# The first transform step as two 64-column matmuls with signed tables, and weight stores issued from ScalarE's queue

## The chip, the cores and the metric

The kernel runs on one core of a Trainium2 chip. The metric is the device time of one execution in microseconds (us), from the first to the last instruction with what lies around them. The engines are TensorE (PE; its weight loads are shown as PEld), VectorE (DVE), ScalarE (ACT), GpSimd (POOL) and SyncE (SP), which here only issues DMAs.

## The reference

A long convolution, and two feed-forward layers on its result, for S = 12480 tokens of width D = 128:

```python
h_filt = (np.maximum(pos_emb @ w1, 0) @ w2) * np.exp(-0.01 * pos)[:, None]
u = x * v
y = irfft(rfft(u, n=2*S) * rfft(h_filt, n=2*S))[:S]       # per channel
a = x * y
h = a @ w_in;  a = (h * clip(h + 3, 0, 6) / 6) @ w_out    # d_ff = 2048
h = a @ w_in2; out = where(h > 0, h, exp(min(h, 0)) - 1) @ w_out2
```

All arrays are float32 on the host.

## The kernel before

The convolution is done with matmuls, as a Fourier transform of length 196 x 128 in two steps. The input is folded beforehand: position i and its mirror image lie side by side, so that the transform works on the sums (f = 0) and the differences (f = 1) of such pairs, 64 of each.

**Opening.** `filter_hidden` (L262) makes the hidden values of the filter: matmuls on TensorE, one VectorE instruction that applies relu and window (L269), and the sums and differences (L274, on VectorE or GpSimd). It writes them to `Rf`.

**First steps of the transform.** `first` (L293) transforms four channels at a time: four fp32 matmuls (L296), each with 98 x 128 stationary values (64 sums and 64 differences of one channel) and a 98 x 198 table `t1` as the moving operand. The result `pa` (PSUM; the pool `ps` has four buffers) has the sums in partitions 0 to 63 and the differences in 64 to 127. Both went through the same table, and the differences need its columns with real and imaginary part exchanged and one sign changed. So the result is written to SBUF by three instructions: L300 copies the upper half (ScalarE, 792 elements), L301 copies one part of the lower half (ScalarE, 396), L302 multiplies the other by -1 (VectorE, 396). `first` runs 32 times in what is called stage 1 here (16 times for the signal into `Au`, `au` in the profile, and 16 for the filter into `Ar`, part of `qb`), and 16 times more in stage 3.

The signal's input comes from `signal` (L252): three GpSimd instructions (L255 multiplies x and v, L257 and L258 make sums and differences) into one of three buffers. Its loads are issued by SP: `ld` from `in_xc` (L215) and `qb` from `in_vc` (L206).

**The stages.** Stage 1 is the list `steps` (L407). Stage 2, `second_all(0)`, runs over groups of four frequencies, two groups at a time: `second_r` (L324; ScalarE copies its result, L327), `second_u` (L316), `second_h` (L331); then per group ScalarE copies half of the result `z` (L336, `ta`), VectorE makes two products (L338, `tb` and `tc`), and GpSimd their sums (L344). Stage 3 (L420) runs `third` for the first half of the channels (PE L353, a ScalarE copy L357, two VectorE instructions L359) in turn with `first` and `signal` for the second half. Stage 4 is `second_all(1)`. Then come `third` for the second half, `fourth` (L452) and the feed-forward layers (from L514 on; matmuls L575 and L619), which take most of the time.

`fourth` has matmuls with 64 stationary columns (99 x 64) that write to partitions 0 to 63 or 64 to 127 of `y`; the two halves are issued in turn by its inner loop.

**The weights.** The feed-forward weights arrive as 64-bit floats, and VectorE makes 32-bit floats of them in 32 jobs: `weight_steps` (L147) is a generator with three steps a job (L172 to L174; L176 and L177; L181 and L182), of integer and float instructions on 256 columns. After the second step of job k it issues the store of job k-1 to DRAM (L162, from `rs`, three buffers) and the load of job k+2 (L157), both on SP's queue. `convert(n)` (L191) takes n steps on average, and is called after each `first` in stage 1 (1.1 steps), after each group of stage 2 (1.5), each round of stage 3 (1.5) and each group of stage 4 (0.6). Every engine and queue works through its instructions in the order in which this program issues them; there is no other scheduler.

The lines that the change touches:

Of the kernel before, what the change touches and what calls it, by code (L numbers as in the profile page):

```python
# [9 lines left out]
F32 = mybir.dt.float32  # L10
# [5 lines left out]
ALU = mybir.AluOpType  # L16
# [5 lines left out]
H1 = N1 // 2  # L22
NK = H1 + 1
HN = N2 // 2
# [24 lines left out]
def tables():  # L49
    n1, k1, k2 = np.arange(H1), np.arange(NK), np.arange(N2)  # L50
    i, m, a = np.arange(HN), np.arange(NM), np.arange(H1) - 2 * SHIFT - 1
    w = 2 * np.pi * (np.outer(n1 - SHIFT, k1) % N1) / N1
    t1 = np.stack([np.cos(w), -np.sin(w)], axis=2)
    k = k1[:, None] + N1 * k2
    w = np.pi * (((2 * i + 1)[:, None, None] * k) % (2 * L)) / L
    gm = np.concatenate([np.cos(w), np.sin(w)], axis=0)

    w = 2 * np.pi * (np.outer(k2, m) % N2) / N2
    c, s = np.cos(w), np.sin(w)
    cs = np.stack([  # L60
        np.concatenate([c[:, :HN], s[:, 1:HN], c[:, HN:]], axis=1),
        np.concatenate([c[:, :1], s[:, 1:HN], c[:, 1:]], axis=1),
    ], axis=1)
    w = 2 * np.pi * (np.outer(k1, a) % N1) / N1
    pa = np.stack([np.cos(w), -np.sin(w), np.sin(w), np.cos(w)], axis=1)
    ends = (m == 0) | (m == HN)
    w = 2 * np.pi * np.outer(k1, m) / L - np.where(ends, np.pi / 4, 0.0)
    c = np.outer(np.where((k1 == 0) | (k1 == H1), 1.0, 2.0) / L, np.where(ends, np.sqrt(0.5), 1.0))
    pm = np.stack([np.cos(w), np.sin(w)], axis=2) * c[:, :, None]
    win = folded(np.exp(-0.01 * np.arange(S, dtype=np.float32))[:, None])[:, 0].transpose(0, 2, 1)  # L70
    return [np.ascontiguousarray(z, dtype=np.float32) for z in (t1, gm, cs, pa, pm, win)]


def folded(z):

    z = np.pad(z, ((0, SP - S), (0, 0))).reshape(H1, N2, -1)
    return np.stack([z[:, HN:], z[:, HN - 1::-1]], axis=1).transpose(0, 3, 1, 2)
# [3 lines left out]
def tile_kernel(ctx, tc, xc, vc, xT, posT, w1_d, w2_d, moe_w, t1_d, gm_d, cs_d, pa_d, pm_d, win_d, outT):  # L81
    nc = tc.nc
    w_dram = [nc.dram_tensor(f"w_scratch{i}", (128, FF), F32, kind="Internal").ap() for i in range(4)]
# [15 lines left out]
    const = sctx.enter_context(tc.tile_pool(name="const", bufs=1, side="right"))  # L99
# [4 lines left out]
    WC = 256  # L104
# [30 lines left out]
    def load_pos(n):  # L135
        for c in (slice(a * H1, b * H1) for a, b in list(zip(edges, edges[1:]))[n]):
            nc.sync.dma_start(pos_t[:, c], posT[:, c])

    load_pos(slice(0, 3))
    t1 = const.tile([H1, 2 * NK], F32, name="t1")  # L140
    nc.scalar.dma_start(t1, t1_d)
    cs = const.tile([128, 2 * N2], F32, name="cs")
    nc.scalar.dma_start(cs, cs_d)
    nc.scalar.dma_start(w2s.rearrange("p h x -> p (h x)"), w2_d)
# [2 lines left out]
    def weight_steps():  # L147
        v = nc.vector
        jobs = [(i, c) for i in range(4) for c in range(0, FF, WC)]
        raws = [spare[:, :2 * WC], spare[:, 2 * WC:4 * WC], late[:, 3 * VT:]]  # L150
        e, rs = spare[:, 4 * WC:5 * WC], [spare[:, (5 + i) * WC:(6 + i) * WC] for i in range(3)]
        ei = e.bitcast(I32)

        def load(k):
            if k < len(jobs):
                i, c = jobs[k]
                nc.sync.dma_start(raws[k % 3].bitcast(I64), moe_w[i][:, c:c + WC])  # L157

        def store(k):
            if k >= 0:  # L160
                i, c = jobs[k]
                nc.sync.dma_start(w_dram[i][:, c:c + WC], rs[k % 3])  # L162

        load(0)
        load(1)
        yield
        for k in range(len(jobs)):
            r32 = raws[k % 3].rearrange("p (n t) -> p n t", t=2)
            lo_w, hi_w = r32[:, :, 0].bitcast(U32), r32[:, :, 1].bitcast(I32)
            r = rs[k % 3]  # L170
            ri = r.bitcast(I32)
            v.tensor_scalar(ei, hi_w, 20, 0x7FF, op0=ALU.logical_shift_right, op1=ALU.bitwise_and)  # L172
            v.tensor_scalar(ri, hi_w, 0xFFFFF, 0x100000, op0=ALU.bitwise_and, op1=ALU.bitwise_or)
            v.tensor_scalar(ei, ei, 896, 1151, op0=ALU.max, op1=ALU.min)  # L174
            yield
            v.scalar_tensor_tensor(r, lo_w, 2.0 ** -32, ri, op0=ALU.mult, op1=ALU.add)  # L176
            v.tensor_scalar(ei, ei, -896, 2 ** 23, op0=ALU.add, op1=ALU.mult)  # L177
            store(k - 1)
            load(k + 2)
            yield  # L180
            v.scalar_tensor_tensor(ei, hi_w, -0x80000000, ei, op0=ALU.bitwise_and, op1=ALU.bitwise_or)  # L181
            v.scalar_tensor_tensor(r, r, 2.0 ** -20, e, op0=ALU.mult, op1=ALU.mult)  # L182
            yield
        store(len(jobs) - 1)

    weights = weight_steps()
# [106 lines left out]
    def first(src, to):  # L293
        pa = ps.tile([128, DC, 256], F32, tag="ps", name="pa")
        for j in range(DC):
            nc.tensor.matmul(  # L296
                pa[:, j, :2 * NK], lhsT=src[:, j].rearrange("p f i -> p (f i)"), rhs=t1, start=True, stop=True
            )
        pv = pa[:, :, :2 * NK].rearrange("p d (k r) -> p d k r", r=2)
        nc.scalar.copy(to[:HN], pv[:HN])  # L300
        nc.scalar.copy(to[HN:, :, :, 0], pv[HN:, :, :, 1])  # L301
        nc.vector.tensor_scalar(to[HN:, :, :, 1], pv[HN:, :, :, 0], -1.0, None, op0=ALU.mult)  # L302

    def first_u(ut, slot):
        first(ut, Au[:, slot:slot + DC])

    def first_r(c):
        first(Rf[:, c * DC:(c + 1) * DC], Ar[:, c * DC:(c + 1) * DC])
# [127 lines left out]
    pa = lds.tile([NK, 2, 2 * H1], F32, name="pa")  # L436
# [255 lines left out]
```

## Time and profile before

| | |
|---|---|
| Median of 3 runs | 1466.36 us (1464.81 to 1466.78) |
| Profiled execution, its own time | 1466.04 us |
| Its span, first to last instruction | 1464.3 us |
| PE busy | 1410.5 us, 96% |
| DVE busy | 1267.9 us, 87% |
| ACT busy | 1021.4 us, 70% |
| POOL busy | 507.1 us, 35% |
| Mean granted TensorE clock | 0.987 |

Times in the rows are in us from the start of the span unless marked ns. The shares are means over stages that have different limits: the feed-forward layers begin at about 369 us, and the change lies wholly before that. fp32 matmuls appear as two records each, so the 128 matmuls of `first` in stage 1 are 256 records.

### The profile page before, as it was taken

The page shows a single profiled execution, that of the slowest core. Times are in us where ns is not written, and L with a number is a line of the kernel's source. Part 1 is how long each engine was busy: PE and PEld are TensorE (multiplying, and loading weights), DVE is VectorE, ACT ScalarE, POOL GpSimd, SP SyncE. Part 2 cuts the span into 40 slices and gives each one's busy share as a digit, 9 for nine tenths or more (in the row PEclk, how much of TensorE's full clock was granted, in tenths as well). Part 3 has the DMA queues.
Part 4 walks back from the last instruction along what each step waited for, and adds up shares of the span by engine and source line. Part 5 has one row for each costly group of instructions (what it writes and reads, how often), then busy time and mean ns, then how long its engine had stood idle before and what let it go on. Part 6 is the DMA issues. An engine that isn't in the chain of part 4 may idle for free.

```text
span 1464.3 us, 21243 instructions
## 1 busy us (share of the span) xinstructions
PE 1410.5 (96%) x8030; PEld 1247.5 (85%) x8030; DVE 1267.9 (87%) x1449; ACT 1021.4 (70%) x1216; POOL 507.1 (35%) x438
## 2 busy tenths in 40 slices
PE   6879888899999999999999999999999999999998
PEld 6879878899888888888888888888888888888887
DVE  6989799879899888888888888888888888888887
ACT  1763344246788777777777777777777777777776
POOL 6645775801242222222222222222222222222223
PEclk8899999999999999999999999999999999999999
DMA  5654255406300000000000000000000000000000
GB/s 175 189 153 151 86 147 155 123 8 171 101 1 7 7 8 7 0 8 7 7 7 8 7 7 1 7 8 8 7 7 8 7 1 8 7 8 7 8 7 14
DMA packets 36659, 60.62 MB, mean 41 GB/s; under 512 B 4291, under 2 KB 17997, under 8 KB 36429
## 3 DMA queue, kind: packets, MB, share of 16 engines
q1 hardware_dynamic: 36044, 58.88, 13.5%
q8 instruction: 63, 1.03, 0.3%
q10 hardware_dynamic: 512, 0.39, 0.1%
q14 instruction: 40, 0.32, 0.1%
HBM read 48.67 MB, written 10.58 MB: 40 GB/s over the span
## 4 chain that ended last, share of the span: by engine, by line
PE 79%; DVE 14%; issue 3%; DMA 1%; POOL 1%; ACT 1%; SPq 0%; DVEq 0%; POOLq 0%; ACTq 0%
PE h L575 36%; PE o L619 36%; PE y L461 3%; PE q L353 2%; DVE tb L338 2%; DVE tc L338 1%; DVE qb L359 1%; DVE qb L174 1%; DVE qb L181 1%; DVE au L302 1%; DVE qb L177 1%; DVE qb L172 1%; DVE qb L176 1%; DVE qb L274 1%; DVE qb L302 1%
## 5 line engine op out<-in xcount | busy, mean ns | idle before, releaser
L619 PE MATMUL o<-gs,w 128*128 128x480 f32 x2496 | 580.1, 380 | 0.2 <-DVE gs L609 0.2
L588 POOL TENSOR_SCALAR a<-a 128x960 f32<-128x960 f32 x208 | 288.2, 1385 | 743.8 <-ACT a L587 703.0
L619 PEld LDWEIGHTS o<-gs,w 128*128 128x128 f32 x2496 | 469.3, 188 | 75.0 <-DVE gs L609 0.6
L609 DVE TENSOR_TENSOR gs<-g,gs 128x960 fp32r<-128x960 f32 x416 | 485.9, 1168 | 4.4 <-ACT gs L604 4.4
L604 ACT CAST gs<-g 128x960 fp32r<-128x960 f32 x416 | 412.5, 992 | 56.5 <-DVE g L596 54.7
L596 DVE SCALAR_TENSOR_TENSOR g<-a,h 128x960 f32<-128x960 f32 x208 | 239.9, 1154 | 139.2 <-ACT a L585 139.1
L575 PE MATMUL h<-xs,w 128*128 128x480 f32 x1248 | 305.6, 381 | 2.4 <-POOL w L490 1.9
L575 PE MATMUL h<-x,w 128*128 128x480 f32 x1248 | 304.0, 379 | 0.0
L575 PEld LDWEIGHTS h<-xs,w 128*128 128x128 f32 x1248 | 234.3, 188 | 40.1 <-POOL w L490 2.3
L587 ACT ACTIVATE a<-h 128x960 f32<-128x960 f32 x208 | 202.5, 974 | 94.3 <-PE h L575 93.4
L575 PEld LDWEIGHTS h<-x,w 128*128 128x128 f32 x1248 | 233.9, 188 | 38.5 <-issue 0.4
L585 ACT ACTIVATE a<-h,three 128x960 f32<-128x960 f32 x208 | 221.0, 1062 | 62.6 <-PE h L575 62.2
L598 DVE SCALAR_TENSOR_TENSOR g<-a,h 128x960 f32<-128x960 f32 x208 | 238.5, 1147 | 0.2 <-POOL a L588 0.2
L344 POOL TENSOR_TENSOR au<-tb,tc 128x256 f32<-128x256 f32 (+3 forms) x108 | 89.6, 860 | 55.8 <-DVE tc L338 52.1
L336 ACT COPY ta<-z 128x512 f32<-128x512 f32 (+3 forms) x54 | 29.7, 551 | 74.3 <-PE z L331 46.2
L296 PE MATMUL pa<-t,qb 98*128 98x198 f32 x256 | 57.4, 391 | 15.3 <-DVE au L302 6.0
L296 PEld LDWEIGHTS pa<-t,qb 98*128 98x128 f32 x256 | 53.3, 229 | 19.3 <-issue 5.9
L353 PE MATMUL q<-cs,au 128*99 128x128 f32 x512 | 60.5, 278 | 7.5 <-DVE qb L359 7.1
L353 PEld LDWEIGHTS q<-cs,au 128*99 128x99 f32 x512 | 58.3, 173 | 10.0 <-issue 7.2
L490 POOL TENSOR_TENSOR w<-w 128x512 fp32r<-128x512 f32 x16 | 24.6, 1539 | 103.4 <-ACT w L489 61.4
L331 PE MATMUL z<-qb 128*128 128x128 f32 x396 | 51.6, 277 | 0.5 <-DVE qb L359 0.5
L255 POOL TENSOR_TENSOR ld<-ld,qb 98x512 f32<-98x512 f32 x32 | 41.7, 1303 | 22.9 <-DMA qb<-in_vc 22.9
(60 smaller groups left out, 1021.5 us busy)
## 6 DMA issues: line engine op xcount, KB each, us to landing
ld<-in_xc SPq DMA_DIRECT2D x32, 196.0 KB
qb<-in_vc SPq DMA_DIRECT2D x32, 196.0 KB
out_T<-y SPq DMA_DIRECT2D x26, 240.0 KB
xt<-in_xT SPq DMA_DIRECT2D x31, 195.0 KB
qb<-in_mw SPq DMA_DIRECT2D x22, 256.0 KB
qb<-in_gm SPq DMA_DIRECT2D x22, 256.0 KB
ld<-in_gm SPq DMA_DIRECT2D x22, 256.0 KB
w_scratch<-qb SPq DMA_DIRECT2D x32, 128.0 KB
```

The source lines that it names most:

```text
L296: nc.tensor.matmul(pa[:, j, :2 * NK], lhsT=src[:, j].rearrange("p f i -> p (f i)"), rhs=t1, start=True, stop=True)
L344: nc.gpsimd.tensor_tensor(out=Au[:, slots(hf), k0:k0 + nk, r], in0=m1[:, :, :nk, r], in1=m2[:, :, :nk, 1 - r], op=op)
L353: nc.tensor.matmul(q[:NK, r, j], lhsT=Au[:, s0 + j, :, r], rhs=cs[:, r * N2:(r + 1) * N2], start=True, stop=True)
L575: nc.tensor.matmul(h[:, j, :TT], lhsT=wslice(2 * m - 2, a, 2 * u + j), rhs=x[:, b], start=i == 0, stop=i == 2)
L585: nc.scalar.activation(a, h[:, :, :TT], AF.Relu, bias=three)
L587: nc.scalar.activation(a, h[:, :, :TT], AF.Exp)
L588: nc.gpsimd.tensor_scalar(a, a, 1.0, 0.0, op0=ALU.min, op1=ALU.max)
L596: nc.vector.scalar_tensor_tensor(g, a, 6.0, h[:, :, :TT], op0=ALU.min, op1=ALU.mult)
L598: nc.vector.scalar_tensor_tensor(g, a, -1.0, h[:, :, :TT], op0=ALU.add, op1=ALU.max)
L604: nc.scalar.copy(t[:, 0], g)
L609: nc.vector.tensor_tensor(out=t[:, 1], in0=g, in1=t[:, 0].bitcast(F32), op=ALU.subtract)
L619: nc.tensor.matmul(o[:, :TT], lhsT=wslice(2 * m - 1, a, 2 * u + j), rhs=gs[:, b, j], start=u == 0 and j == 0 and i == 0, stop=u == NU - 1 ...
```

## The change

The table `t1` gets a second half for the differences, with the parts exchanged and the signs set. `first` issues for each channel two matmuls with 64 stationary columns, one for the sums into partitions 0 to 63 and one for the differences into 64 to 127, each with its own half of the table as the moving operand (198 columns as before). One ScalarE copy takes the result to SBUF; L301 and L302 are gone. Apart from that, the weight stores are issued on ScalarE's DMA queue instead of SP's.

```diff
@@ tables
-    t1 = np.stack([np.cos(w), -np.sin(w)], axis=2)
+    c, s = np.cos(w), np.sin(w)
+
+    t1 = np.stack([np.stack([c, -s], axis=2), np.stack([-s, -c], axis=2)], axis=1)
@@ tile_kernel
-    t1 = const.tile([H1, 2 * NK], F32, name="t1")
-    nc.scalar.dma_start(t1, t1_d)
+    t1 = const.tile([H1, 2, 2 * NK], F32, name="t1")
+    nc.scalar.dma_start(t1.rearrange("p f k -> p (f k)"), t1_d)
@@ weight_steps, store
-                nc.sync.dma_start(w_dram[i][:, c:c + WC], rs[k % 3])
+                nc.scalar.dma_start(w_dram[i][:, c:c + WC], rs[k % 3])
@@ first
         for j in range(DC):
-            nc.tensor.matmul(
-                pa[:, j, :2 * NK], lhsT=src[:, j].rearrange("p f i -> p (f i)"), rhs=t1, start=True, stop=True
-            )
-        pv = pa[:, :, :2 * NK].rearrange("p d (k r) -> p d k r", r=2)
-        nc.scalar.copy(to[:HN], pv[:HN])
-        nc.scalar.copy(to[HN:, :, :, 0], pv[HN:, :, :, 1])
-        nc.vector.tensor_scalar(to[HN:, :, :, 1], pv[HN:, :, :, 0], -1.0, None, op0=ALU.mult)
+            for f in range(2):
+                nc.tensor.matmul(
+                    pa[f * HN:(f + 1) * HN, j, :2 * NK], lhsT=src[:, j, f], rhs=t1[:, f], start=True, stop=True
+                )
+        nc.scalar.copy(to, pa[:, :, :2 * NK].rearrange("p d (k r) -> p d k r", r=2))
```

## Rows read from the trace of the kernel before

**Rows 1.** The page: VectorE's busy tenths in 40 slices of 36.6 us.

```profile
DVE  6989799879899888888888888888888888888887
```

**Rows 2.** Busy us by engine in stages 1, 2 and 3; then clock, DMA share, GB/s.

```profile
core 0: us, PE busy (x) PEld busy (x) DVE busy (x) ACT busy (x) POOL busy (x), PEclk, DMA share, GB/s
35.90:103.20 67.30, 54.95 (x257) 51.33 (x257) 64.88 (x113) 47.57 (x63) 37.38 (x40) 0.85 0.60 175
106.80:165.00 58.20, 54.53 (x470) 53.20 (x469) 57.62 (x103) 21.28 (x30) 34.60 (x38) 1.00 0.46 140
177.30:240.40 63.10, 52.38 (x371) 49.81 (x369) 59.28 (x102) 30.14 (x48) 44.07 (x50) 0.96 0.44 124
```

**Rows 3.** VectorE's L302 alone in stages 1 and 3.

```profile
35.90:103.20 67.30, 22.57 (x32) 0.85 0.60 175
177.30:240.40 63.10, 9.20 (x16) 0.96 0.44 124
```

**Rows 4.** ScalarE's instructions of stage 1: busy, mean ns, idle before them and releaser.

```profile
L301 ACT COPY qb<-pa 64x396 f32<-64x396 f32 x16 | 13.5, 845 | 0.2
L300 ACT COPY qb<-pa 64x792 f32<-64x792 f32 x16 | 13.5, 844 | 8.7 <-PE pa L296 8.5
```

**Rows 5.** Timeline of VectorE: one instruction beside GpSimd's, then with GpSimd idle.

```profile
50.57 1.27 DVE L172 TENSOR_SCALAR qb<-late 128x256 int32<-128x256 int32 x1
...
99.66 0.43 DVE L176 SCALAR_TENSOR_TENSOR qb<-qb 128x256 f32<-128x256 uint32 x1
...
101.23 0.57 DVE L302 TENSOR_SCALAR au<-pa 64x396 f32<-64x396 f32 x1
101.84 0.29 DVE L172 TENSOR_SCALAR qb<-late 128x256 int32<-128x256 int32 x1
...
102.57 0.57 DVE L302 TENSOR_SCALAR au<-pa 64x396 f32<-64x396 f32 x1
...
106.84 0.69 DVE L338 TENSOR_TENSOR tb<-z,ta 128x512 f32<-128x512 f32 x1 [3.03 <-ACT ta L336]
```

**Rows 6.** The last instruction of each weight job in stage 1.

```profile
L182 DVE SCALAR_TENSOR_TENSOR qb<-qb 128x256 f32<-128x256 f32 x11 | 6.0, 549 | 0.4
```

**Rows 7.** L461 alone, PE and PEld: one half (323 us), then both halves in turn.

```profile
323.10:325.00 1.90, 1.90 (x23) 1.90 (x24) 1.00 0.00 0
339.00:368.90 29.90, 29.89 (x709) 29.73 (x707) 1.00 0.57 151
```

**Rows 8.** Timeline of TensorE in stage 3, and where L461 ends.

```profile
193.19 1.51 PE L296 MATMUL pa<-t,late 98*128 98x198 f32 x8
...
196.37 1.51 PE L296 MATMUL pa<-t,late 98*128 98x198 f32 x8
...
365.78 3.45 PE L461 MATMUL y<-ti,qb 99*64 99x97 f32 x77
369.17 3.08 PE L575 MATMUL h<-xs,w 128*128 128x480 f32 x13
```

**Rows 9.** What SP's queue waited for, 36 to 99 us: total, times, longest.

```profile
SPq L162 <- DVE qb L182: 35.9, 10, 5.5
```

**Rows 10.** Five busy microseconds of stage 1 for the DMA engines.

```profile
60.00:65.00 5.00, 4.97 (x15) 5.00 (x16) 4.84 (x8) 1.43 (x3) 3.83 (x4) 0.50 0.97 292
```

**Rows 11.** DMA issues on ScalarE's queue, timeline; the size of the table's load.

```profile
0.73 0.65 ACTq L133 DMA_DIRECT2D qb<-in_win  x1
1.41 0.32 ACTq L141 DMA_DIRECT2D t<-in_t  x1
...
t<-in_t ACTq DMA_DIRECT2D x1, 75.8 KB
```

**Rows 12.** One round of stage 2, timeline of ACT, DVE and PE.

```profile
137.69 1.01 ACT L327 COPY qb<-r 128x1024 f32<-128x1024 f32 x1 [1.16 <-PE r L324]
...
139.31 0.95 DVE L182 SCALAR_TENSOR_TENSOR qb<-qb 128x256 f32<-128x256 f32 x1
140.07 1.95 PE L331 MATMUL z<-qb 128*128 128x128 f32 x16
...
141.21 0.59 ACT L336 COPY ta<-z 128x512 f32<-128x512 f32 x1 [2.51 <-PE z L331]
...
143.82 0.68 DVE L338 TENSOR_TENSOR tb<-z,ta 128x512 f32<-128x512 f32 x1
```

## The prediction

> **What bounds the kernel now.** I read the page first, for the slices: VectorE is nearly full in most of the first ten, which hold all that the change touches [rows 1]. Then the windows by stage: VectorE is busy for 64.9 of 67.3 us in stage 1, 57.6 of 58.2 in stage 2, 59.3 of 63.1 in stage 3, while TensorE, GpSimd and ScalarE have 17% to 52% to spare in stages 1 and 3 [rows 2]. So there VectorE's queue sets the end, and a microsecond off VectorE is worth one until another engine is full. The rest of the span, from 369 us, has none of the changed lines and only moves.
>
> **Removed from VectorE.** L302 took 22.6 us in stage 1 and 9.2 in stage 3 [rows 3]: 31.8 us, the most that can be won there. What remains in stage 1 is the weight conversion: 64.9 - 22.6 = 42.3 us [rows 2, 3] for 11 jobs [rows 6]. That price doesn't hold still. With GpSimd idle, L176 to L182 take 1.57 us (99.66 to 101.23) and L172 to L174 0.73 (101.84 to 102.57), 2.3 us a job; but L172 took 1.27 us beside a GpSimd instruction and 0.29 without [rows 5]. Eleven jobs alone are 25.3 us, so 17.0 of the 42.3 are waiting. GpSimd worked 37.4 of 67.3 us [rows 2]; spread evenly, 23.5 us of conversion lay beside it, so each such us cost 0.72. L302 reads PSUM and shows no such stretch: 0.575 us each in stage 3 [rows 3], 0.57 with GpSimd idle [rows 5]. Without it all of GpSimd's 37.4 us can fall on conversion: 25.3 + 0.72 x 37.4 = 52.3 us, against 42.3 if the price stays. Stage 1 on VectorE: from 67.3 to 52.3 us at worst, 15 us won, and 22.6 at best.
>
> The Trainium skill (SBUF — State Buffer, "SBUF: two separate sides") says why: VectorE's two-port instructions and GpSimd's lock a shared pair of ports against each other, and the loser waits for the whole instruction. The 1.27 beside 0.29 us agree [rows 5]. Without that rule the gain would be put at 22.6 us; with it at 15.
>
> **Can the others keep that pace in stage 1?** TensorE: 240 records of L296 fall there; eight streamed back to back take about 1.35 us (1.51 from start to modelled end, less the tail of 0.165) [rows 8], so 40 us, and up to 10 more because the granted clock is at its lower level, 1.2 GHz, for part of the time (mean 0.85, 15% of 67.3 us) [rows 2]. GpSimd 37.4 us. ScalarE pays 0.84 us for the copy of 792 elements, whatever the partitions, and loses L301's 0.84 [rows 4]: 27 us for 32. DMA: 175 GB/s x 67.3 us = 11.8 MB [rows 2], 40 us at the 292 GB/s that five full microseconds reached [rows 10]. All are under 52, none by much, and they hand work to each other. I take 55 to 57 us, not 52. What follows is the wait for the first products: 106.84, 3.0 us of it idle [rows 5], because stage 2 waits for the last L302. Now TensorE need not wait for VectorE there, which gives back 1 or 2 us. Stage 1: 12 us gained (bounds 5 and 22.6).
>
> **Added to TensorE: twice the matmuls.** Do two halves of the array work at once? `fourth` has the same form: 64 columns, halves in turn. With one half alone 23 records took 1.90 us, 83 ns each; with both in turn 709 took 29.9 us, 42 ns each [rows 7]. So a pair costs what one cost, with different stationary data in each half and, in part, different moving data. I price `first` at its old stream time plus one unpaired record at the end: 1.35 + 0.17 = 1.51 us. The bounds: nothing extra, and everything twice (a rival, below). In stage 1, where calls follow each other, the extra record pairs with the next call.
>
> In stage 3 `first` alternates with `third`, so each round has two changes between half and full array. A round of third and first takes 3.18 us (193.19 to 196.37) [rows 8]; 14 of these, two lone firsts and 2 us of L331 are 49 us on TensorE. After L461's halves the next full matmul starts at 369.17, before the modelled end of the last half, 369.23 [rows 8]: a change is cheap, 0.1 us. With unpaired records (16 x 0.17) and 32 changes it is 55 us.
>
> The Trainium skill (TensorEngine Tiling (Array Packing), "Key Properties") says that changing the tiling mode drains TensorE, which speaks against this change. If each of the 32 changes waited out the tail of 0.165 us [rows 8], the sum would be 57 us instead of 55. The rows show no full drain.
>
> VectorE in stage 3: 59.3 - 9.2 = 50.1 us [rows 2, 3], plus about 4 for more conversion beside GpSimd (44 us busy in a shorter stage), 54. So the two engines meet at 54 to 57 us, and with some waiting between them I take 58 instead of 63.1. Stage 3: 5 us gained (bounds 0 and 9.2).
>
> **Moved: the stores.** SP stood 35.9 us in ten waits of L162 for L182 [rows 9], with the load of weights and the loads of v and x queued behind. The load behind it waits for nearly the same VectorE work (its buffer is free after L181), so SP gains little: 0.35 us of issue a job. But the wait now stands in ScalarE's queue, ahead of its next copies. In stage 1 ScalarE can't run ahead of VectorE by more than about a job, nor VectorE by more than three (the buffers of `rs`); four PSUM buffers and ScalarE's 40 us of slack take that up, which is part of why I took 55 to 57.
>
> Stage 2 is where it could hurt: the store of job k comes after the second `ta` of a round and ahead of the next L327, while its L182 ends at 140.26; L327 ran at 137.69 [rows 12]. So L327 moves 3 us later. The issue costs ScalarE 0.32 to 0.65 us [rows 11], so L327 ends at 140.26 + 0.4 + 1.01 = 141.7; L331, which needs it, then takes 1.14 us to the first `ta` (140.07 to 141.21), and `ta` 0.59: ready at 143.5, before the product at 143.82 [rows 12]. Covered by 0.3 us. If the issue costs 0.65 or more, or each hand-over 0.1 more, some ten rounds pay 0.1 to 0.5 us each. I take 0.5 us in all (bounds 0 and 5). In stages 3 and 4 the job stored ended at least one group earlier: nothing.
>
> The table's load grows from 75.8 KB [rows 11] to twice that, 0.4 us at 175 GB/s, beside the opening loads: 0.2.
>
> **Sum.** -12 - 5 + 0.5 + 0.2 = -16.3 us on the profiled execution's 1466.04, 1449.7; the runs' median is 0.3 above it: 1450.
>
> **Rivals.**
> - *The freed time goes into new waits.* The ScalarE store ties TensorE, ScalarE and VectorE into one lockstep, and loads or GpSimd set the pace: stage 1 gains 5, stage 3 gains 1, stage 2 loses 3. For it: GpSimd and the DMA engines have little slack once 67 us are 55. Against it: VectorE is busy for 96% of stage 1 now [rows 2], so what the others wait for is mostly VectorE. Time: 1463, or 1457 if only one part holds.
> - *The halves don't overlap.* With 198 columns moving for each half, all records run one after the other. Stage 1 then has 480 records x 0.168 = 81 us on TensorE, 91 with the clock's 10, against 67.3; stage 3 14 x (3.18 + 1.35) + 7.4 = 71 against 63. Slower by 22 to 32: 1488 to 1498. It decides once a pair costs over 0.28 us instead of 0.17 (67.3 us over 240 pairs). Against it: 42 beside 83 ns [rows 7].
> - *Slower by the store's wait alone*: each round of stage 2 would have to pay over 1.7 us to eat the gain. The chain above is short of its cover by at most 0.5.
>
> **How the numbers follow.** Forecast, faster by 9 to 25 us (1441 to 1457): 0.69. New waits (1457 to 1463.4): 0.14. Within 0.2% (2.9 us, about what can be told from no change): 0.06. Slower: 0.11, 0.08 of it halves that don't overlap. Faster thus 0.83. The range reaches from the best sums that I believe (17 and 8 us gained) to the case where new waits take most: 1441 to 1462.
>
> **What would show it.** L296 has 768 records of 98x64, with 84 ns a record where they follow each other; over 0.16 falsifies the pairing. VectorE in stage 1 has only conversion, at more than 2.3 us a job, and ends near 90. The first products of stage 2 start near 95 instead of 106.84. Stage 2 keeps 58 us; if it grew, ScalarE would be seen waiting for L182 ahead of L327. Stage 3 takes about 58 us, with TensorE over 90% busy. The prediction is wrong if `ta` becomes VectorE's releaser in stage 2, if GpSimd waits longer for loads of v than before, or if the clock stays low in stage 1 because TensorE pauses oftener.

## The result and the profile after

The changed kernel takes 1442.3 us (median of 4 runs, 1441.5 to 1443.4) against 1466.6 for the kernel before (4 runs, 1464.8 to 1467.0): ratio 0.9837, interval 0.9820 to 0.9854, 24.2 us faster. The forecast was 16.3 us faster, 1450, with 1441 to 1462 as its range. The profiled execution took 1442.7 us, its span 1440.9. One execution at a granted clock of 0.655 (1980 us, of the kernel with only the stores moved) is left out below, because all others ran at 0.98 to 1.00.

To see where the 24 us come from I cut each trace at the same seven events: the first weight step on VectorE, the first product `tb` of stage 2, the last product of that stage (a `tc`), the first `tb` of stage 4, the first `fourth`, the first L575, the end. The last column is a run of the changed kernel with its table loaded in two pieces (below). It is nearly the same program, so it shows how far two executions differ.

| us | before | after | near-twin of after |
|---|---|---|---|
| opening, to the first weight step | 36.5 | 32.3 | 32.2 |
| stage 1, to the first `tb` | 70.4 | 54.1 | 56.0 |
| stage 2, to the last product | 72.8 | 72.9 | 72.8 |
| stage 3, to the next `tb` | 62.6 | 59.4 | 56.4 |
| stage 4, to `fourth` | 80.8 | 80.6 | 80.6 |
| `fourth`, to L575 | 46.1 | 46.6 | 46.8 |
| feed-forward, to the end | 1095.1 | 1094.9 | 1093.7 |

Stage 1 gives 14 to 16 us, stage 3 gives 3 to 6, the opening 4, the rest nothing beyond what the twin differs by. VectorE's slices on the page of the changed kernel, now of 36.0 us (compare [rows 1]):

```profile
DVE  7999669788898888888888888888888888888887
```

Most of stage 3 lies in the fifth and sixth slice, which are at 6; before, it lay in the sixth and seventh, at 9. VectorE no longer bounds it. The windows of stages 1 to 3 (busy us by engine, then clock, DMA share, GB/s; compare [rows 2]), and below them L299 alone, PE and PEld, in stages 1 and 3:

```profile
32.20:83.90 51.70, 49.04 (x503) 39.81 (x504) 50.56 (x83) 25.41 (x32) 40.33 (x40) 0.93 0.78 226
86.40:147.00 60.60, 56.40 (x483) 54.59 (x482) 57.64 (x103) 21.79 (x30) 37.02 (x41) 1.00 0.44 135
156.00:218.70 62.70, 59.30 (x516) 49.41 (x516) 43.61 (x91) 22.54 (x33) 54.85 (x51) 0.97 0.44 136
```

```profile
32.20:83.90 51.70, 45.94 (x478) 36.84 (x478) 0.93 0.78 226
156.00:218.70 62.70, 27.59 (x256) 18.93 (x256) 0.97 0.44 136
```

Stage 1: VectorE 50.6 of 51.7 us and TensorE 49.0, both nearly full. Stage 3: VectorE down from 59.3 to 43.6 us; TensorE 59.3 and GpSimd 54.9 of 62.7 are what is left.

VectorE in stage 1 (timeline: start, us, line), compare [rows 5]:

```profile
70.13 1.25 DVE L174 TENSOR_SCALAR qb<-late 128x256 int32<-128x256 int32 x1
...
73.11 1.36 DVE L179 TENSOR_SCALAR qb<-qb 128x256 int32<-128x256 int32 x1
...
80.52 0.29 DVE L174 TENSOR_SCALAR qb<-qb 128x256 int32<-128x256 int32 x1
...
82.25 0.42 DVE L184 SCALAR_TENSOR_TENSOR qb<-qb 128x256 f32<-128x256 f32 x1
...
86.42 0.69 DVE L338 TENSOR_TENSOR tb<-z,ta 128x512 f32<-128x512 f32 x1 [2.48 <-ACT ta L336]
```

Once GpSimd has finished its inputs, a whole weight job takes 2.2 us (80.52 to 82.70, where the next begins). With GpSimd working without a pause one job takes 6.2 us, from the L174 at 70.13 to the next at 76.31: L174 1.25 us instead of 0.29, L179 1.36 instead of 0.28. In these 6.2 us GpSimd does exactly two inputs; the two engines wait for each other in turn. The conversion alone now fills the stage.

A round of stage 2 on ScalarE, VectorE and TensorE, compare [rows 12]:

```profile
94.24 0.95 DVE L184 SCALAR_TENSOR_TENSOR qb<-qb 128x256 f32<-128x256 f32 x1
...
95.22 0.35 ACTq L164 DMA_DIRECT2D w_scratch<-qb  x1
95.61 1.01 ACT L327 COPY qb<-r 128x1024 f32<-128x1024 f32 x1 [2.40 <-PE z L316]
...
96.68 2.05 PE L331 MATMUL z<-qb 128*128 128x128 f32 x16 [0.52 <-ACT qb L327]
...
97.93 0.59 ACT L336 COPY ta<-z 128x512 f32<-128x512 f32 x1 [1.30 <-PE z L331]
...
98.76 0.68 DVE L338 TENSOR_TENSOR tb<-z,ta 128x512 f32<-128x512 f32 x1
```

The store goes out at once when L184 ends (95.19), L327 comes behind it, L331 now waits for L327, and `ta` ends at 98.52, before `tb` at 98.76: 0.24 us to spare. The next round's `tb` is 6.16 us after the one of this round, as before.

Three rounds of stage 3 on TensorE, compare [rows 8]:

```profile
164.77 1.56 PE L299 MATMUL pa<-t,late 98*64 98x198 f32 x16
166.26 2.00 PE L353 MATMUL q<-cs,au 128*99 128x128 f32 x16
168.19 1.56 PE L299 MATMUL pa<-t,late 98*64 98x198 f32 x16
```

A round takes 3.42 us, with sixteen half records where eight full ones were. The round in [rows 8] took 3.18, but it holds small waits; the shortest round of the kernel before takes 3.09 (221.51 - 218.42):

```profile
218.42 1.51 PE L296 MATMUL pa<-t,late 98*128 98x198 f32 x8
...
221.51 1.51 PE L296 MATMUL pa<-t,late 98*128 98x198 f32 x8
```

So a round costs TensorE 0.33 us more than before. TensorE doesn't hold this pace to the end of the stage. The chain that ended last (start, us, what) passes to GpSimd at 180.6 us and GpSimd's groups in 160 to 213 us (busy, mean ns, idle before) show it with no gaps:

```profile
177.07 1.93 PE q L353 x16
179.00 1.54 PE pa L299 x16
180.54 0.05 issue
180.59 0.78 POOL late L260
181.37 2.08 POOL ld L257
...
184.28 2.37 POOL late L260
```

```profile
L257 POOL TENSOR_TENSOR ld<-ld,qb 98x512 f32<-98x512 f32 x14 | 19.1, 1364 | 0.0
L260 POOL TENSOR_TENSOR late<-ld 98x256 f32<-98x256 f32 x14 | 18.9, 1350 | 0.0
L259 POOL TENSOR_TENSOR late<-ld 98x256 f32<-98x256 f32 x14 | 12.7, 905 | 1.1
```

Before the change the same 14 differences took 819 ns each:

```profile
L258 POOL TENSOR_TENSOR late<-ld 98x256 f32<-98x256 f32 x14 | 11.5, 819 | 0.0
```

Nothing in them has changed, and the mean of 1350 ns hides two kinds: eight took 0.78 to 0.98 us, six took 1.42 to 2.37. In each of the six, VectorE ran some 1 to 1.6 us of conversion. The longest, from 184.28 to 186.65, holds five conversion instructions of VectorE one behind the other, each as short as with GpSimd idle:

```profile
184.28 2.37 POOL L260 TENSOR_TENSOR late<-ld 98x256 f32<-98x256 f32 x1
184.85 0.28 DVE L174 TENSOR_SCALAR qb<-qb 128x256 int32<-128x256 int32 x1
...
185.78 0.28 DVE L179 TENSOR_SCALAR qb<-qb 128x256 int32<-128x256 int32 x1
```

So here GpSimd does the waiting. In stage 1 of the same run, where conversion has no pauses, the 13 differences took 0.77 to 0.91 us and VectorE did the waiting. What decides which of the two waits, no run shows.

### The profile page after: what moved, and what is told of

It is laid out like the page before. It is cut to its first block, busy times and chain, and to the rows that moved or that the text cites. A ratio compares the mean times of both kernels' runs of the same rounds, so it can differ in the third digit from the quotient of the medians.

```text
span 1440.9 us, 21903 instructions
## 1 busy us (share of the span) xinstructions
PE 1407.4 (98%) x8414; PEld 1229.8 (85%) x8414; DVE 1235.1 (86%) x1401; ACT 990.4 (69%) x1168; POOL 519.8 (36%) x438
## 4 chain that ended last, share of the span: by engine, by line
PE 80%; DVE 12%; POOL 3%; issue 2%; ACT 1%; DMA 1%; SPq 0%; DVEq 0%; POOLq 0%; ACTq 0%
PE h L575 37%; PE o L619 37%; PE y L461 3%; PE q L353 3%; DVE tb L338 2%; DVE tc L338 1%; DVE qb L178 1%; POOL au L344 1%; DVE qb L176 1%; POOL late L260 1%; DVE qb L183 1%; DVE qb L276 1%; POOL ld L257 1%; DVE qb L179 1%; DVE qb L174 1%
## 5 line engine op out<-in xcount | busy, mean ns | idle before, releaser
L604 ACT CAST gs<-g 128x960 fp32r<-128x960 f32 x416 | 412.6, 992 | 56.4 <-DVE g L596 54.7
L575 PE MATMUL h<-xs,w 128*128 128x480 f32 x1248 | 306.2, 381 | 3.0 <-POOL w L490 1.9
L575 PE MATMUL h<-x,w 128*128 128x480 f32 x1248 | 304.1, 379 | 0.0
L575 PEld LDWEIGHTS h<-xs,w 128*128 128x128 f32 x1248 | 234.9, 189 | 40.6 <-POOL w L490 2.3
L575 PEld LDWEIGHTS h<-x,w 128*128 128x128 f32 x1248 | 234.1, 188 | 38.2 <-issue 0.4
L331 PE MATMUL z<-qb 128*128 128x128 f32 x396 | 53.3, 283 | 4.2 <-ACT qb L327 4.2
L299 PE MATMUL pa<-t,qb 98*64 98x198 f32 x512 | 51.2, 356 | 6.3 <-POOL qb L259 3.7
L359 DVE TENSOR_TENSOR qb<-q,tb 99x512 f32<-99x512 f32 (+2 forms) x68 | 41.4, 654 | 17.9 <-ACT tb L357 17.7
L299 PEld LDWEIGHTS pa<-t,qb 98*64 98x64 f32 x512 | 40.0, 147 | 17.2 <-POOL qb L259 4.4
```

Source lines behind the costliest of these rows:

```text
L299: nc.tensor.matmul(pa[f * HN:(f + 1) * HN, j, :2 * NK], lhsT=src[:, j, f], rhs=t1[:, f], start=True, stop=True)
L575: nc.tensor.matmul(h[:, j, :TT], lhsT=wslice(2 * m - 2, a, 2 * u + j), rhs=x[:, b], start=i == 0, stop=i == 2)
L604: nc.scalar.copy(t[:, 0], g)
```

## The experiments

My theory, from the traces: the gain is L302's removal from VectorE; the halves pair and cost nothing but the two changes a round between full and half array; the move of the stores is neutral; what bounds stage 1 now is conversion stretched by GpSimd, and in stage 3 GpSimd stretched by conversion. The rivals: the stores' move is what freed something; the halves cost time that another gain hides; TensorE or the loads bound stage 1. All ratios below are to the kernel before, measured beside it.

**The two parts apart.** The changed kernel with its stores back on SP:

```
-                nc.scalar.dma_start(w_dram[i][:, c:c + WC], rs[k % 3])
+                nc.sync.dma_start(w_dram[i][:, c:c + WC], rs[k % 3])
```

> The changed kernel with the weight stores back on SP's queue: the halves and the single copy alone. Theory A (VectorE's relief from L302 is the gain, the stores' queue is neutral): 1441 to 1446 us, stage 1 as short as in the changed kernel within 2 us, SP waiting for the last instruction of a weight job again. Theory B (the gain comes from SP no longer standing in that wait, so that loads of v and x start earlier): 1452 us or more, GpSimd waiting for loads of v for 15 us or more in stage 1. The opening: if the wider table's load made it 4 us shorter, the first weight step starts near 32.3 us here as well.

It took 1442.0 us (1439.0 to 1447.9), 0.9844 (0.9821 to 0.9868): the same as the changed kernel. Its stage 1 is longer (57.2 us, 3 more and not within the 2 that I expected), its stage 3 shorter (54.4) than in the trace of after; since the near-twin differs from after by 2 and 3 us in these stages, only the sum is shown, and the sum is nothing that these runs can tell.

The change took L301 off ScalarE together with L302, and no run separates the two. But VectorE was idle for only 2.4 of the 67.3 us of stage 1 [rows 2], so relief of ScalarE alone could have won no more than that there.

The kernel before with the stores on ScalarE's queue, and nothing else:

```
-                nc.sync.dma_start(w_dram[i][:, c:c + WC], rs[k % 3])
+                nc.scalar.dma_start(w_dram[i][:, c:c + WC], rs[k % 3])
```

> The kernel before with only the stores moved to ScalarE's queue. Theory A: 1464 to 1469 us, the same as before, with VectorE still full in stage 1. Theory B: 1450 us or less. If the wait in ScalarE's queue costs something when VectorE is the bound, up to 5 us slower than before, seen as ScalarE waiting for the last instruction of a weight job. The opening has the old table: the first weight step near 36.5 us if the table's load made the difference, near 32.3 us if it was the change of queue or chance.

1461.8 us (median of 11 runs, 1459.6 to 1464.8), 0.9973 (0.9959 to 0.9987): 4 us faster and 2 us below my range for a neutral move, so not quite nothing while L302 is there. Where these 4 us come from stays open. The wait on SP didn't go away, as the prediction had said:

```profile
SPq L157 <- DVE qb L181: 40.0, 11, 5.9
```

The load behind the store waits for VectorE's L181 (total, times, longest us) as long as the store had waited for L182 [rows 9]. So nearly all of the 24 us are the first step's.

**What the halves cost.** The changed kernel with whole matmuls of 128 columns and the narrow table, and still one ScalarE copy; the exchange and the sign of the lower half are left out:

```
...
-            for f in range(2):
-                nc.tensor.matmul(
-                    pa[f * HN:(f + 1) * HN, j, :2 * NK], lhsT=src[:, j, f], rhs=t1[:, f], start=True, stop=True
-                )
+            nc.tensor.matmul(
+                pa[:, j, :2 * NK], lhsT=src[:, j].rearrange("p f i -> p (f i)"), rhs=t1, start=True, stop=True
+            )
```

> Matmuls with 128 stationary columns and the old table, and the single ScalarE copy; stores on ScalarE's queue. It leaves out the exchange of parts and the change of sign for the differences, so that it has the relief of VectorE without the halves. Theory A with the predicted price of the halves (one unpaired record of 0.17 us and two changes of 0.1 us for each call in stage 3, nothing in stage 1): 1437 to 1442 us, a round of third and first 3.2 us instead of 3.4. If the halves cost more than that, for instance by keeping stage 1 longer: below 1436 us. If the halves themselves speed TensorE up: above 1444 us.

1445.7 us (1440.2 to 1447.4), 0.9857 (0.9835 to 0.9879): not faster than the halves. It lies in the range that I had given to halves that speed TensorE up, but they don't: whole matmuls take rounds of down to 3.14 us in stage 3, halves 3.42. By stage: 53.8, 72.8, 59.5 and 80.6 us from stage 1 to 4, against 54.1, 72.9, 59.4 and 80.6 after the change. Its profiled opening was late (36.5), of which more below. Twice the number of matmuls costs nothing that the end sees.

The changed kernel with the two loops exchanged, so that one half's eight records are issued before the other's:

```
-        for j in range(DC):
-            for f in range(2):
+        for f in range(2):
+            for j in range(DC):
```

> The changed kernel with the two loops exchanged: all four channels' sums first, then all four channels' differences, so that records of one half follow each other. If two halves overlap only where their records stand next to each other in the queue: the records run 0.168 us apart but at the seams, a call takes about 2.4 us on TensorE instead of 1.34 to 1.5, stage 1 is 75 to 85 us long and the kernel takes 1470 to 1490 us. If TensorE overlaps halves in any order: 1442 us as before.

1446.6 us (1444.5 to 1448.6), 0.9870 (0.9849 to 0.9892). It loses 4 us, not the tens that I expected; in its profile stage 3 takes 62.4 us instead of 59.4. TensorE in stage 3 (timeline):

```profile
168.41 2.28 PE L299 MATMUL pa<-t,late 98*64 98x198 f32 x16
170.62 2.00 PE L353 MATMUL q<-cs,au 128*99 128x128 f32 x16
172.55 2.28 PE L299 MATMUL pa<-t,late 98*64 98x198 f32 x16
```

A call takes 2.21 us here (168.41 to 170.62) instead of 1.49 (164.77 to 166.26), not the double. The record starts show why: four records alone, 0.168 us apart; then, over four steps of 0.168 us, two records in each; then four alone again. Twelve steps instead of eight. So some records of the second half ran beside the first half's last four, though they were issued behind them. In stage 1, where calls follow each other, the 54.5 us that it takes show no loss.

**What bounds stage 1 now.** The changed kernel with one GpSimd instruction an input instead of three; sums and differences are left out:

```
-        nc.gpsimd.tensor_tensor(out=xt, in0=xt, in1=vts[n % 3], op=ALU.mult)
...
-        nc.gpsimd.tensor_tensor(out=ut[:, :, 0], in0=xt[:, :, 0], in1=xt[:, :, 1], op=ALU.add)
-        nc.gpsimd.tensor_tensor(out=ut[:, :, 1], in0=xt[:, :, 0], in1=xt[:, :, 1], op=ALU.subtract)
+        nc.gpsimd.tensor_tensor(out=ut, in0=xt, in1=vts[n % 3], op=ALU.mult)
```

> The changed kernel with one GpSimd instruction instead of three for each piece of the signal: the product of x and v goes straight to the buffer that the first step reads, and the sums and differences are left out. Theory A (after the change VectorE and GpSimd hold each other up at the ports that they share: the price of a weight job, and the length of GpSimd's instructions in stage 3, come from that): GpSimd's work in stage 1 falls from 40 to about 21 us, a weight job from 4.2 to below 3.3 us, stage 1 from 54.1 to 48 to 51 us where TensorE (46 us of matmuls, part at 1.2 GHz) and the loads take over; stage 3 from 59.4 to 54 us, where TensorE is full. In all 1430 to 1435 us. Theory C (the loads or the stores' wait set the pace now): both stages keep their length within 2 us, 1440 to 1444.

1428.4 us, 0.9744 (0.9720 to 0.9767), 1.6 below my range. Its stage 1 in the columns of the windows:

```profile
32.90:80.00 47.10, 47.10 (x510) 38.94 (x509) 33.17 (x83) 25.38 (x31) 15.35 (x11) 0.94 0.82 233
```

VectorE does the same 83 instructions in 33.2 us instead of 50.6, though nothing was taken from it: only GpSimd's 40.3 us beside it became 15.4. TensorE is then busy for all of the 47.1 us, so it stood 4 to 5 us behind VectorE as the next bound. In this run stage 1 takes 49.0 us and stage 3 53.0.

**What bounds stage 3.** The differences of stage 3 moved from GpSimd to VectorE, the planner's RATE for stages 2 and 3 shifted by 0.2 jobs of weights a round, and both together; the two edits:

```
-        nc.gpsimd.tensor_tensor(out=ut[:, :, 1], in0=xt[:, :, 0], in1=xt[:, :, 1], op=ALU.subtract)
+        e = nc.vector if n >= NC + 2 else nc.gpsimd
+        e.tensor_tensor(out=ut[:, :, 1], in0=xt[:, :, 0], in1=xt[:, :, 1], op=ALU.subtract)
...
-    RATE = (1.1, 1.5, 1.5, 0.6)
+    RATE = (1.1, 1.3, 1.7, 0.6)
```

Both:

> The changed kernel with two moves towards what is idle now: in stage 3 the differences of the signal are made by VectorE instead of GpSimd, and 3.6 steps of the weight conversion go from stage 2 (1.3 steps a group instead of 1.5), where VectorE is full, to stage 3 (1.7 a round instead of 1.5). Theory A: stage 3 falls from 59.4 to 54 to 57 us, bounded by TensorE, and stage 2 from 72.9 to 69 to 71, bounded by VectorE and TensorE; 1433 to 1439 us. If TensorE or the loads bound stage 3 already: 1440 to 1444. If VectorE in stage 3 can't take 12 us more: slower than 1444.

The differences alone:

> The changed kernel with the differences of stage 3 moved from GpSimd to VectorE, and nothing else: one of the two edits of the run before it that gained 4 us. If GpSimd is the bound of stage 3 after the change, the stage falls from 59.4 to 54 to 55 us and the time to 1437 to 1439. If the stage was bound by VectorE or by TensorE instead, it stays at 59 us or grows, and the time is 1442 to 1446.

The shift alone:

> The changed kernel with the other edit alone: the planner puts 1.3 instead of 1.5 jobs of weights on each round of stage 2 and 1.7 instead of 1.5 in stage 3. If VectorE still bounds stage 2, that stage falls from 72.9 to 69 us; stage 3, which GpSimd bounds, has no more of GpSimd's work, but its steps meet more of VectorE's, so it is 59 to 62 us: 1438 to 1442 in all. If stage 2 does not depend on VectorE's weight work, it stays at 73 us and the time is 1442 to 1446.

Both: 1438.1 us, 0.9810 (0.9785 to 0.9835). The differences alone: 1435.2 (1434.9 to 1436.9), 0.9800 (0.9783 to 0.9817), 7 us below the changed kernel (I had expected 3 to 5), and the best of the kernels that leave nothing out. The shift alone: 1441.5, 0.9838 (0.9814 to 0.9862), nothing. It does take stage 2 from 72.9 to 69.0 us, so VectorE is still the bound there, but stage 4 grows by 2.5 us and stage 3 keeps 57.9, and the sum is within what one run differs from another. With the differences on VectorE stage 3 takes 52.5 us; its windows row, and the same stage of the changed kernel:

```profile
159.30:211.80 52.50, 51.41 (x482) 43.78 (x481) 44.56 (x101) 21.01 (x30) 40.80 (x32) 1.00 0.54 162
```

```profile
159.30:218.70 59.40, 56.01 (x482) 46.59 (x481) 41.58 (x86) 21.09 (x30) 51.55 (x46) 0.97 0.46 143
```

TensorE goes from 94% to 98% busy, and GpSimd has 11.7 us to spare. GpSimd was the bound of stage 3 in the profile after the change, and with that gone TensorE is. The two are near each other, though. In the run with the stores on SP, all of GpSimd's work was there, and yet TensorE set the pace: each round took 3.42 us.

```profile
164.00:216.00 52.00, 50.45 (x461) 42.45 (x458) 38.94 (x85) 20.37 (x29) 48.33 (x47) 0.97 0.50 151
```

GpSimd's differences took 0.81 us each there (its sums 1.27 instead of 0.91).

**How near the store's wait came.** Each store cut into four on ScalarE's queue, so that its issue takes four times as long:

```
-                nc.scalar.dma_start(w_dram[i][:, c:c + WC], rs[k % 3])
+                for o in range(0, WC, WC // 4):
+                    nc.scalar.dma_start(w_dram[i][:, c + o:c + o + WC // 4], rs[k % 3][:, o:o + WC // 4])
```

> The changed kernel with each weight store cut into four, so that ScalarE issues four DMAs of 64 columns for one of 256. If the store's place in ScalarE's queue is covered in stage 2 by some 0.2 to 0.3 us and no more: three issues of 0.34 us more make L327, L331 and the copies behind them 1.0 us later, and each of some ten rounds 0.75 to 0.85 us longer than 6.16; stage 2 grows by 7 to 9 us, the kernel to 1449 to 1453. If it is covered with room, or doesn't stand on that chain: within 2 us of 1442.

1465.6 us (1462.0 to 1468.0), 0.9999 (0.9983 to 1.0015): all of the gain is gone, 12 us more than I expected. Stage 2 takes 87.7 us instead of 72.9, and a full round 7.46 instead of 6.16 in five cases of nine, and 7.9 to 8.6 in the others:

```profile
131.51 0.69 DVE L339 TENSOR_TENSOR tb<-z,ta 128x512 f32<-128x512 f32 x1 [1.22 <-ACT ta L337]
...
134.15 1.77 ACTq L165 DMA_DIRECT2D w_scratch<-qb  x4
135.97 1.01 ACT L328 COPY qb<-r 128x1024 f32<-128x1024 f32 x1 [3.68 <-DMA w_scratch<-qb]
...
138.97 0.69 DVE L339 TENSOR_TENSOR tb<-z,ta 128x512 f32<-128x512 f32 x1 [1.22 <-ACT ta L337]
```

The four issues take 1.77 us instead of 0.35; that is 1.4 more against a cover of 0.24, and `tb` waits 1.22 us for `ta`. In stage 1 the stores make trouble as well: ScalarE's copies wait 19.5 us in five waits named after the store's transfer, and the stage takes 61.0 us. Part of the loss there may be the transfers in smaller pieces and not the issue; I didn't separate these.

**The opening.** Does the wider table shorten it? In the chain of the kernel before, then of after (start, us, what):

```profile
2.11 8.31 DMA qb<-in_posT
...
10.47 6.17 PE pr L265 x32
```

```profile
2.12 6.87 DMA qb<-in_posT
...
9.04 2.00 PE pr L267 x16
```

The load on the chain lands 1.4 us earlier, and the 16 records that VectorE's second L271 needs take 2.00 us, where the 32 of before took 6.17. So the third L271 starts at 13.2 us, the third L269 of before at 16.7. From there it is 19 us of the same work to the first weight step in both, and the kernel before has one L302 of 0.57 us more ahead of it. Three kernels tell whether the table does this. The kernel before with the whole wide table loaded, of which the first half is used:

```
+    t1 = np.stack([t1, t1], axis=1)
...
-    t1 = const.tile([H1, 2 * NK], F32, name="t1")
-    nc.scalar.dma_start(t1, t1_d)
+    t1 = const.tile([H1, 2, 2 * NK], F32, name="t1")
+    nc.scalar.dma_start(t1.rearrange("p f k -> p (f k)"), t1_d)
...
```

> The kernel before with a table twice as wide in memory and in its load, of which the matmuls use the first half as before; nothing else is changed. If the wider load is what makes the opening 2 to 5 us shorter (first weight step at 31.5 to 34.3 us with the wide table, at 36.2 to 36.5 with the narrow one): first weight step at 31 to 34.5 us, the kernel 2 to 5 us faster than before, 1461 to 1464. If the opening differs for another reason: 36 us and 1466.

The kernel before with the table wide in DRAM and half of it loaded, in rows of the old length:

```
...
-    nc.scalar.dma_start(t1, t1_d)
+    nc.scalar.dma_start(t1[:, 0], t1_d[:, :2 * NK])
...
```

> The kernel before with the table twice as wide in DRAM, of which only the first half is loaded, in rows of the old length. If only the width of the transfer matters, the first weight step stays at 36.2 to 36.5 us and the time at 1465 to 1468. If the longer input by itself moves the opening, it comes at 35 us, as with the whole wide table (35.09), and the time is 1463 to 1464.

The changed kernel with the table loaded in two halves:

```
-    nc.scalar.dma_start(t1.rearrange("p f k -> p (f k)"), t1_d)
+    for f in range(2):
+        nc.scalar.dma_start(t1[:, f], t1_d[:, f * 2 * NK:(f + 1) * 2 * NK])
```

> The changed kernel with its table of 151.6 KB loaded by two DMAs of half the width each instead of one. If the opening is shorter after the change (first weight step of VectorE at 32.3 us instead of 36.5) because the wider rows of this one load let the loads queued beside it pass faster, the first weight step falls back to 35 to 36.5 us and the time to 1445 to 1447. If the width is not the cause, the first weight step stays at 31.5 to 33 us and the time at 1441 to 1444.

1463.8 us, 0.9987 (0.9972 to 1.0002); 1465.2 us, 1.0004 (0.9990 to 1.0019); 1441.4 us, 0.9844 (0.9823 to 0.9865). None of the three differs measurably from the kernel that it was made from. In their profiles the first weight step comes at 35.1, 33.4 and 32.2 us. The second has the loads of the kernel before, and yet in its chain the first load lands early:

```profile
2.12 7.29 DMA qb<-in_posT
...
9.46 2.00 PE pr L266 x16
```

So the opening differs by 3 us between executions whose loads are the same, and no width of the table is shown to matter. Of the 4.2 us, 0.6 is the L302 that no longer stands ahead of the first weight step; the other 3 or so I can't give to the change. That the openings of the changed kernels came at 31.5 to 34.3 us, in the nine profiles with half matmuls and the wide table, and those of the other five at 33.4 to 36.5, may be luck of single profiles or not; it stays open.

## Why the prediction was right, and where not

- *VectorE bounds stages 1 and 3, and L302 is what can be won there*: right. With L302 gone 24 us are gone, 4 of them in the opening, which isn't explained. The stores alone make 4 us before the change, and after it none that the runs can tell.
- *Stage 1, 12 us*: too small; it was 14.4 and 16.3 in the two profiles of the table (13.2 with the stores on SP). The step that failed is "I take 55 to 57 us, not 52". The sum for VectorE was 52.3 us at worst, and the stage took 51.7, to 83.9 us, where the conversion pauses; the near-twin and the run with the stores on SP took as long to the same point. What differs between the three is the wait for the first products, 2.5, 4.4 and 5.5 us, against 3.0 before: the 1 or 2 us that I had counted on there did not come. The first products came at 86.4 instead of near 95, 4 of these 9 us from the opening. I had added 3 to 5 us because four other resources came near it; TensorE came nearest, at 49.0, and still didn't add to it. Two of my fears went the other way. TensorE's granted clock was at 1.2 GHz for only the first 7 us of the stage (mean 0.93 instead of 0.85 [rows 2]; 1.00 from 60 to 65 us, where [rows 10] had 0.50), and GpSimd waited 4.6 us for loads of v instead of 17.6.
- *All of GpSimd's time falls on conversion, at 0.72 us each*: the mechanism is right, the price a little high. 11.7 jobs at 2.2 us and one L276 of 1.5 leave 23.3 of the 50.6 us, and these over GpSimd's 40.3 are 0.58. (I had counted 11 jobs before the change too, where 81 conversion instructions, seven a job, make 11.6.) The price isn't a constant: with one GpSimd instruction an input the same sum gives 0.4. That run shows the cause and not only the sum. The Trainium skill (SBUF — State Buffer, "SBUF: two separate sides") puts it down to a pair of ports that VectorE and GpSimd lock against each other; the 1.25 beside 0.29 us agree, and it was worth 15 instead of 22.6 us in the forecast.
- *Two halves cost what one full matmul cost*: right. The records start in pairs, 3 to 7 ns apart, the pairs 0.167 us apart, 84 ns a record as forecast.
- *An unpaired record of 0.17 us and two cheap changes a round in stage 3*: the sum was near and its parts weren't. All sixteen records pair, so no record is left over, and the 0.33 us of 3.42 beside 3.09 lie at the two changes, 0.16 each, where I had put 0.1. The Trainium skill (TensorEngine Tiling (Array Packing), "Key Properties") has the array drain at such a change; the trace agrees, since 0.16 us is as much as the tail of 0.165 us in [rows 8]. My "The rows show no full drain" read one change, behind L461, where the next record started before a modelled end. In the profile after the change the cost was hidden, since GpSimd sets the end of the stage: the run with whole matmuls has the same 59.5 us.
- *Stage 3, 58 us and TensorE with VectorE at the bound*: the size came out (5 us forecast; 3.2, 6.2 and, with the stores on SP, 8.1 in three profiles), but partly by luck, since the bound was another. VectorE, put at 54 us, was busy for 43.6; TensorE was full as forecast in one of the three, with the stores on SP; in the profile after the change GpSimd ended last. I let GpSimd's 44 us add 4 us to VectorE and forgot that GpSimd can be the one that waits: six of its differences took 1.42 to 2.37 us beside conversion, and 44.1 us became 54.9.
- *The store's chain in stage 2 is covered by 0.3 us*: right; 0.24 was left and the stage kept its time, so the 0.5 us that I had put for ten rounds was not lost. The run with four stores shows how near it was: 1.4 us more of issue, and most of it came out of every round. Its 1.3 us and more a round come near the 1.7 that the rival needed.
- *The halves don't overlap; new waits take the gain*: the first needed over 0.28 us a pair; it was 0.167. Of the second a small part came: GpSimd's longer differences in stage 3, and in two of the three profiles 1.4 and 2.5 us more of waiting for the first products than before.
- *The opening loses 0.2*: in the profiles compared it gained 4.2 us, of which only 0.6 is explained. About half of the 8 us by which the forecast was too small lies there.

## What to carry to other kernels

Where two engines slow each other, an instruction taken off one is worth less than its time there and then shows up on the other: look at both before you say which is the next bound, and in more than one profile, since a near-tie can fall either way. A sum of one engine's work that was already a worst case needed no margin here for its neighbours being nearly as full: 51.7 us came of 52.3, where 3 to 5 us of margin had been added. A wait put into the queue of a lightly used engine is free as long as what stands behind it has cover, and that cover is to be measured: 0.24 us here, eaten several times over by three more issues.

## What the runs showed of the hardware

- Half records that aren't issued side by side still pair when they are near: with eight of one half ahead of eight of the other, four pairs formed, by the order of issue each of the fifth to eighth record of the first half with one of the second (twelve steps of 0.168 us instead of eight or sixteen). That only four paired in each call, I can't explain.
- The two changes a round between full and half array cost TensorE 0.33 us together (a round of 3.42 us beside 3.09).
- GpSimd's subtraction of 256 elements took 0.78 to 0.98 us in eight of 14 cases of one stage and 1.42 to 2.37 in six, with nothing in it changed; in the longest, VectorE ran five conversion instructions in a row at their shortest, 0.28 to 0.41 us. In another stage VectorE was the one that waited: L174 took 1.25 us instead of 0.29.
- Four stores of a quarter each held ScalarE's queue for 1.77 us where one held it for 0.35.
